# Eight places for late gate/up outputs, one product for the fifth class, gate/up grouped by side, and another written-out order

## The chip, the cores and the metric

The kernel runs on one core of one Trainium2 chip. The metric is the device time of one execution in microseconds. The core has five engines with an instruction queue each: PE (matrix products), ACT and DVE (elementwise work, and all copies out of PE's result memory, PSUM), POOL, and SP, which here only issues transfers.

## The reference

x is [2048, 640]; F is 1536. All arrays are bf16.

```python
xn = layernorm(x)                                   # over the 640 columns, no scale or shift
A  = irfft2(rfft2(xn) * (w_r + 1j * w_i))           # a filter in the two-dimensional spectrum
B  = ((xn @ w_gate) * (xn @ w_up)) @ w_down         # a bilinear gated layer, no activation
out = x + A + B
```

## The kernel before

**Blocks and names.** The 2048 rows are 16 blocks of 128. A block is normalised in place: statistics by two bn_stats and one aggregate on DVE (bn, ag), or by a sum and a sum of squares on ACT (sm at line 740, sq at line 749, for the blocks in `aset`: block 3 and blocks 6 to 15); then a square root on ACT (sd), a reciprocal and one tensor_scalar on DVE (rs, mul). Blocks 0 to 3 are transposed on PE (T0, line 818) and copied out (eT0); blocks 4 to 15 are transposed by a DMA on SP (xt).

**The gated layer.** A unit is a strip of one, two or four blocks and one or two column groups of 128 (ft 0 to 11). For each unit PE makes two GU tasks into one PSUM bank each (lines 948 and 968), ACT or DVE copies each out as bf16 (eG, lines 683 and 684), and one DVE product (H, lines 984 and 985) writes the hidden layer. There are 50 units, in the order of their readiness. The copies go to `GBF`, three places of two outputs in turn (`rr = ui % 3`), so an eG must wait for the H that read the place before. In units of four blocks one GU task is gate and the other up; in the smaller units each task computes gate and up for one column group.

**The spectrum.** DVE builds sums and differences of the normalised blocks in five groups (S1 to S5); PE turns them (R, line 908), ACT and DVE copy them out (eR). When all 16 are there, for each of 16 steps t: D (line 1025), its copy (eD), C (line 1045), the filter products WM on DVE with the weights of a group of two steps, negated copies NS on POOL, and, for each pair of steps, SM, JA and JB, then four inverse products IA (lines 1116, 1118) and their copies. WM has four products of 256 elements (line 1062) for classes one to four and two of 130 elements (line 1068) for the fifth class. Then 16 inverse steps I (line 1147) with copies eI, five DVE steps V1 to V5 for each of five groups of blocks, and the last transform IV (line 1236), which adds into the same PSUM bank as the down products ACC (line 1224).

**The end.** FINA copies a bank out on ACT, FIN adds x on DVE, SP stores. Block 15 is done in three pieces.

**Order.** Nothing is scheduled at run time. Every piece of work is a task; `_PLAN` lists all 976 as (number of the task in the order the code creates it, engine 0 to 4 = PE, ACT, DVE, POOL, SP, PSUM bank or -1). `replay` puts each engine's tasks in its queue in that order, and `compute_waits` derives the semaphore waits from buffers read and written. So each engine runs its list strictly in order, and a task that waits holds up all behind it on that engine. Gate load and x loads are issued by SP; the second half of block 0 and the up load of ft 0 and 1 by ACT. PE begins with 40 dummy products (`warm`) and, after T0_0, 12 small ones (`fill`).

**Buffers of filter weights.** The weights of two steps are loaded with 8 transfers (12 for the first) into one of three places; a place is free when the WM of its two earlier steps are done. The down weights (`WD`) lie over the table `TI`, which IA reads.

## Time and profile before

| what | value |
|---|---|
| median of 3 runs | 198.14 us (198.12 to 198.24) |
| span of the profiled execution | 196.1 us |
| PE busy | 191.5 us |
| DVE busy | 176.8 us |
| ACT busy | 136.7 us |
| POOL busy | 27.8 us |
| bytes moved by DMA | 23.75 MB |

The span goes from the first to the last instruction of the program on the core; the runs' time has some microseconds of start and end around it. Busy times of PE rest on modelled ends of its matmuls. A line number names the Python line that emitted the instruction; copies by ACT and DVE have one line each (683 and 684) whatever they copy.

### The profile page before, as it was taken

Reading aid. Unit: us, or ns where it says so; the run is one execution under the profiler, and the core shown is the slowest. Engines: PE = TensorE matmul, PEld = TensorE weight load, DVE = VectorE, ACT = ScalarE, POOL = GpSimd, SP = SyncE. Lnnn points to the kernel's source line nnn. Section 1 sums busy time; section 2 is a strip of 40 time slices with the busy share of each in tenths; the row PEclk is TensorE's granted clock in tenths of the full one; section 3 lists DMA queues with packets and bytes.
Section 4 is the critical chain, followed back from the end, with each engine's and each line's share of the span. In section 5 each row is a group of like instructions: output and inputs, shape, how many; then the busy total and the mean of one; then the engine's idle time right before and its main releaser. Section 6 shows DMA issues by size and latency. Waiting matters only on the chain.

```text
span 196.1 us, 4290 instructions
## 1 busy us (share of the span) xinstructions
PE 191.5 (98%) x1609; PEld 123.1 (63%) x1625; DVE 176.8 (90%) x392; ACT 136.7 (70%) x299; POOL 27.8 (14%) x54
## 2 busy tenths in 40 slices
PE   8999999999999999999999999999999999999995
PEld 8898645445454455556555556557777777777774
DVE  3899999999999889999899999994999999999823
ACT  3197999999957779999989999967505343333130
POOL 1000000000000004545172254460000000000000
PEclk9999999999999999999999999999999999999999
DMA  6999995426318432541451402004301334044422
GB/s 168 306 326 369 392 180 119 116 54 134 84 37 231 183 86 55 133 117 48 110 157 47 132 5 69 0 3 132 105 0 40 97 100 152 15 137 134 134 70 67
DMA packets 29667, 23.75 MB, mean 121 GB/s; under 512 B 10448, under 2 KB 27600, under 8 KB 29520
## 3 DMA queue, kind: packets, MB, share of 16 engines
q1 hardware_dynamic: 28848, 23.08, 41.6%
q10 hardware_dynamic: 800, 0.41, 0.7%
q8 instruction: 13, 0.21, 0.4%
q14 instruction: 6, 0.05, 0.1%
HBM read 18.89 MB, written 2.62 MB: 110 GB/s over the span
## 4 chain that ended last, share of the span: by engine, by line
PE 60%; DVE 19%; issue 6%; ACT 6%; SPq 4%; DMA 4%
PE ps L1224 27%; PE ps L948 21%; ACT arena L683 4%; SPq L677 4%; DMA arena<-in_A_x_dram 4%; DVE arena L984 3%; PE ps L1147 2%; DVE arena L861 2%; PE ps L1236 2%; PE ps L1025 2%; PE ps L1116 2%; PE ps L1045 2%; DVE arena L799 2%; DVE arena L860 2%; DVE arena L895 1%
## 5 line engine op out<-in xcount | busy, mean ns | idle before, releaser
L683 ACT ACTIVATE arena<-ps 128x512 bf16<-128x512 f32 (+6 forms) x243 | 117.3, 530 | 47.3 <-PE ps L1236 21.6
L948 PE MATMUL ps<-arena 128*128 128x512 bf16 x404 | 94.9, 379 | 0.9
L948 PEld LDWEIGHTS ps<-arena 128*128 128x128 bf16 x420 | 39.0, 98 | 41.1 <-ACT arena L683 0.9
L1224 PE MATMUL ps<-arena 128*128 128x320 bf16 (+2 forms) x396 | 57.2, 295 | 0.0
L1224 PEld LDWEIGHTS ps<-arena 128*128 128x128 bf16 x396 | 37.5, 98 | 13.4
L1062 DVE TENSOR_TENSOR arena<-ps,arena 128x256 bf16<-128x256 f32 x64 | 22.7, 418 | 1.4 <-PE ps L1045 1.1
L1077 POOL COPY arena<-arena 128x126 bf16<-128x126 bf16 x16 | 8.9, 556 | 104.1 <-DVE arena L1068 104.1
L984 DVE TENSOR_TENSOR arena<-arena 128x512 bf16<-128x512 bf16 x42 | 17.9, 425 | 0.5
L968 PE MATMUL ps<-arena 128*128 128x128 bf16 (+1 forms) x160 | 13.8, 246 | 0.0
L968 PEld LDWEIGHTS ps<-arena 128*128 128x128 bf16 x160 | 12.2, 98 | 1.3 <-issue 0.2
L1079 POOL TENSOR_SCALAR arena<-arena 128x130 bf16<-128x130 bf16 x16 | 11.8, 740 | 0.0
L1263 DVE TENSOR_TENSOR arena<-arena 128x640 bf16<-128x640 bf16 x15 | 7.1, 486 | 4.8 <-ACT arena L683 4.8
L740 ACT ACTIVATE arena<-arena 128x640 bf16<-128x640 bf16 x11 | 8.3, 757 | 3.6 <-DMA arena<-in_A_x_dram 3.6
L684 DVE CAST arena<-ps 64x321 bf16<-64x321 f32 (+4 forms) x16 | 8.3, 529 | 2.6 <-PE ps L1118 1.1
L1116 PEld LDWEIGHTS ps<-arena 128*128 128x128 bf16 x128 | 7.9, 120 | 3.0 <-issue 0.5
L749 ACT ACTIVATE arena<-arena 128x640 bf16<-128x640 bf16 x11 | 9.3, 844 | 0.0
L1025 PEld LDWEIGHTS ps<-arena 128*128 128x128 bf16 x160 | 7.1, 98 | 3.3 <-issue 0.2
L1116 PE MATMUL ps<-arena 128*128 128x64 bf16 x128 | 8.5, 199 | 0.0
L1068 DVE TENSOR_TENSOR arena<-ps,arena 128x130 bf16<-128x130 f32 x32 | 8.0, 295 | 0.0
L1025 PE MATMUL ps<-arena 128*128 128x64 bf16 (+1 forms) x160 | 8.0, 193 | 0.0
L860 DVE TENSOR_TENSOR arena<-arena 128x768 f32<-128x768 bf16 (+1 forms) x10 | 7.9, 792 | 0.0
L1078 POOL COPY arena<-arena 128x126 bf16<-128x126 bf16 x16 | 7.9, 495 | 0.0
(63 smaller groups left out, 201.2 us busy)
## 6 DMA issues: line engine op xcount, KB each, us to landing
arena<-in_A_x_dram SPq DMA_DIRECT2D x19, 160.0 KB, 2.6
arena<-in_A_w_r_dram SPq DMA_DIRECT2D x30, 80.2 KB, 2.2
arena<-in_A_w_i_dram SPq DMA_DIRECT2D x30, 80.2 KB, 2.2
out_dram<-arena SPq DMA_DIRECT2D x15, 160.0 KB, 1.8
arena<-in_B_w_gate_dram SPq DMA_DIRECT2D x4, 320.0 KB, 5.4
arena<-in_A_x_dram SPq DMA_DIRECT2D x1, 1280.0 KB, 10.1
arena<-c_tf SPq DMA_DIRECT2D x4, 256.0 KB, 10.3
arena<-c_ti SPq DMA_DIRECT2D x2, 512.0 KB, 5.3
```

Source lines behind the costliest of these rows:

```text
L683: return c.e.activation(dst, src, _ACTF.Copy)
L749: return c.e.activation(v_jk, v_x[:, b, :], _ACTF.Square, scale=-1.0, bias=v_m32[:, b:b + 1], accum_out=v_ss[:, b:b + 1])
L860: c.e.tensor_tensor(uo[:, o, :, 0:3, :], v_xb[:, b:b + nt, 0:6:2, :], v_xb[:, b:b + nt, 5:10:2, :], op)
L948: ins = c.e.matmul(ps[:, bk, :], v_gw[:, w, j, ft, :], v_xt[:, j, rows], start=(j == 0), stop=(j == 4))
L968: ins = c.e.matmul(ps[:, bk, w * n:(w + 1) * n], v_gw[:, w, j, ft, :], v_xt[:, j, rows], start=(j == 0), stop=(j == 4))
L984: return c.e.tensor_tensor(v_ht[:, ft0, rows], v_gbf[:, rr, 0, :], v_gbf[:, rr, 1, :], _OP.mult)
L1025: ins = c.e.matmul(ps[:, bk, k * 64:k * 64 + n], v_uq[:, k, t, :], v_fd[:, k * 128 + w * n: k * 128 + w * n + n], start=True, stop=True)
L1062: c.e.tensor_tensor(dst, xh, wv, _OP.mult)
L1077: c.e.tensor_copy(yg[:, :, 65:128], yg[:, :, 257:320])
L1079: return c.e.tensor_scalar(yg[:, :, 128:193], yg[:, :, 256:321], -1.0, None, _OP.mult)
L1116: c.e.matmul(ps[:, bk, 64 * k:64 * k + 64], yl[:, k:512:4], v_ti[:, q, 0, :], start=True, stop=True)
L1224: ins = c.e.matmul(ps[:, bk, 0:sl3.stop - sl3.start], v_ht[:, ft, a * 128:(a + 1) * 128], v_wd[:, ft, sl3], start=(ft == _FT_ORDER[0]), st ...
```

## The change

1. `GBF` keeps three places, and units of blocks 8 to 15 (24 of the 50) go through eight: three in `GBF` and five in the transposed input `XT`, columns 0 to 1023 of its five parts, which hold blocks 0 to 7. A copy to one of those five waits for all GU tasks of blocks 0 to 7.
2. In units of one and two blocks, one GU task now computes gate for both column groups and the other computes up; before, each computed gate and up for one group. H reads the two outputs accordingly.
3. WM's two products of the fifth class become one of 2 x 2 x 65 elements, with the spectrum broadcast over real and imaginary weights.
4. `act_set` becomes (2, 3): block 2's statistics go from DVE (bn, ag) to ACT (sm, sq). This leaves 975 tasks.
5. `fill` has 6 dummy products instead of 12.
6. `_PLAN` is new as a whole.

Parts of the new lists, by the names of the tasks (read from the task numbers), beside those of before:

```
ACT before: x0b, up(0,1), sd0, sd1, eT0_0, sm3, sd2, sq3, sd3, eG2_1, ...
ACT after:  x0b, up(0,1), sd0, sm2, sd1, sq2, eT0_0, sd2, sm3, sq3, sd3, eT0_2, eG2_0, ...
DVE before: ... ag1, mul0, rs1, mul1, eT0_0, eT0_1, eT0_1, eG0_0, eG0_1, H0, bn2, bn2, ag2, ...
DVE after:  ... ag1, mul0, rs1, mul1, eT0_0, rs2, eT0_1, mul2, eT0_1, eG0_0, eG0_1, H0, rs3, mul3, S1_0, ...
PE before:  warm, T0_0, fill, T0_1, GU0, GU0, GU2, GU1, GU1, GU3, GU2, GU3, T0_2, GU4, T0_3, GU4, ...
PE after:   warm, T0_0, fill, T0_1, GU0, GU0, T0_2, GU2, GU1, GU2, T0_3, GU1, GU3, GU3, GU5, GU5, GU4, ...
SP before:  x0a, x1, gate(0,1), gate(2,3), up(2,3), x2, x3, gate(4,5), up(4,5), gate(6,7), ...
SP after:   x0a, x1, x2, x3, gate(0,1), gate(2,3), up(2,3), x4-7, gate(4,5), sm, up(4,5), x8-15, gate(6,7), ...
DVE before: ... WM14, WM15, SM15, JB15, JA15, eIA28, eIA30, eI2, H47, V1_0, ...
DVE after:  ... WM14, WM15, SM15, JA15, JB15, H42, H43, eIA28, eIA31, eG49_0, H44, H45, eI2, H46, V1_0, ...
```

In the plan below, the first three lines of each list are shown.

```diff
@@ -358,6 +358,7 @@
 _S_GROUPS = ((0, 2), (2, 2), (4, 4), (8, 4), (12, 4))
 _V_GROUPS = ((0, 4), (4, 4), (8, 4), (12, 2), (14, 2))
 _NGW = 12
+_NG = 3
 _LAST = ((0, 320), (320, 512), (512, 640))
 _WD_LOADS = ((7, 12), (0, 2), (2, 4), (4, 6), (6, 7))
 _FT_ORDER = (7, 8, 9, 10, 11, 0, 1, 2, 3, 4, 5, 6)
...
-    (11, 4, -1), (12, 1, -1), (13, 4, -1), (171, 1, -1), (170, 4, -1), (8, 3, -1), (18, 2, -1), (172, 4, -1), (173, 4, -1),
-    (19, 2, -1), (20, 2, -1), (27, 2, -1), (28, 2, -1), (21, 1, -1), (14, 4, -1), (22, 2, -1), (29, 2, -1), (10, 0, 0),
-    (0, 3, -1), (30, 1, -1), (23, 2, -1), (24, 0, 2), (31, 2, -1), (32, 2, -1), (26, 2, -1), (25, 1, -1), (15, 4, -1),
...
+    (0, 3, -1), (10, 0, 4), (8, 3, -1), (11, 4, -1), (18, 2, -1), (12, 1, -1), (19, 2, -1), (20, 2, -1), (13, 4, -1),
+    (27, 2, -1), (28, 2, -1), (14, 4, -1), (15, 4, -1), (169, 4, -1), (170, 1, -1), (21, 1, -1), (36, 1, -1), (22, 2, -1),
+    (29, 2, -1), (23, 2, -1), (24, 0, 4), (9, 0, 1), (30, 1, -1), (37, 1, -1), (25, 1, -1), (31, 2, -1), (32, 2, -1),
...
@@ -559,7 +560,7 @@
         lay["TI"] = (lay["WD"][0], 16 * 256)
         b_g = alloc("G", 640)
         b_sm = alloc("SM", 384)
-        b_gbf = alloc("GBF", 6 * 512)
+        b_gbf = alloc("GBF", 2 * _NG * 512)
         b_stat = alloc("STAT", 608)
         b_jk = alloc("JK", 640)
 
@@ -617,7 +618,7 @@
         v_fd = V("FD")
         v_g = V("G")
         v_sm = V("SM").rearrange("p (t n) -> p t n", t=3)
-        v_gbf = V("GBF").rearrange("p (r u n) -> p r u n", r=3, u=2)
+        v_gbf = V("GBF").rearrange("p (r u n) -> p r u n", r=_NG, u=2)
         v_one = nc.const_aps.tensor(1.0, (128, 128), _BF)
         v_us = V("US").bitcast(_F32).rearrange("p (q j b) -> p q j b", q=8, j=5)
         v_tw = v_us[:, :, 1:3, :].rearrange("p q s b -> p s q b")
@@ -698,7 +699,7 @@
             return c.e.memset(v_eps, 1e-5)
         T("eps", "pool", 150.0, em_eps, writes=[(b_ve, None)], prio=-1.0)
         fills = []
-        nfill = opts.get("nfill", 12)
+        nfill = opts.get("nfill", 6)
 
         def em_fill(c):
             bk = bank_of(c.t)
@@ -731,7 +732,7 @@
                 [(b_x, ("s", b0, b0 + nb))], prio=(0.0, opts.get("x1_prio", 0.003), opts.get("x2_prio", 0.02), opts.get("x3_prio", 0.0205), 0.042, 0.06)[gi])
         muls = {}
         sd0 = None
-        aset = set(opts.get("act_set", (3,))) | set(range(opts.get("act_stats", 6), 16))
+        aset = set(opts.get("act_set", (2, 3))) | set(range(opts.get("act_stats", 6), 16))
         for gi, (b0, nb) in enumerate(_LN_GROUPS):
             pbase = 1.0 + 0.05 * gi if gi < 4 else opts.get("ln_prio", 5.9) + 0.05 * (gi - opts.get("ln_lead", 3))
             for b in range(b0, b0 + nb):
@@ -931,16 +932,22 @@
         c_at = [6.3 + opts.get("c_rate", 2.6) * (b0 + nb - 1) for b0, nb, _f0, _f1 in chunks]
         units = sorted((max(c_at[ci], w_at[ft | 1]), ci, ft) for ci in range(len(chunks))
                        for ft in range(chunks[ci][2], chunks[ci][3], 1 if chunks[ci][1] == 4 else 2))
+        gl = []
         for ui, (at_, ci, ft0) in enumerate(units):
             b0, nb = chunks[ci][:2]
             n = 128 * nb
             rows = slice(b0 * 128, b0 * 128 + n)
-            rr = ui % 3
+            late = [u_ for u_ in range(len(units)) if chunks[units[u_][1]][0] >= 8]
+            if ui in late:
+                rr = late.index(ui) % (_NG + 5)
+                rr = (rr + late[0]) % _NG if rr < _NG else rr
+            else:
+                rr = ui % _NG
+            gb = v_gbf[:, rr] if rr < _NG else v_xt[:, rr - _NG, 0:1024].rearrange("p (u n) -> p u n", u=2)
             pu = 40.0 + 0.005 * ui
             pe_ = opts.get("eg_prio", 5.0) + 0.001 * ui
             ph_ = opts.get("h_prio", 5.0) + 0.001 * ui
             for u in range(2):
-                ft = ft0 + u
                 if nb == 4:
                     def em_gu4(c, ft=ft0, w=u, rows=rows):
                         bk = bank_of(c.t)
@@ -953,37 +960,41 @@
                                   (b_xta, ("s", b0 * 128, b0 * 128 + n)), (b_xtb, ("s", b0 * 128, b0 * 128 + n))],
                            prio=pu + 0.001 * u, bank="single", cls="glu")
 
-                    def em_eg4(c, gu=gu, rr=rr, u=u):
-                        return copy_on(c, v_gbf[:, rr, u, :], ps[:, bank_of(gu), :])
+                    def em_eg4(c, gu=gu, gb=gb, u=u):
+                        return copy_on(c, gb[:, u, :], ps[:, bank_of(gu), :])
                     eg = T("eG_%d_%d" % (ui, u), ("act", "dve"), {"dve": _d_dve_psum(n), "act": _d_act(n)}, em_eg4,
-                           writes=[(b_gbf, ("r", 2 * rr + u, 2 * rr + u + 1))], prio=pe_, frees=gu)
+                           writes=[(b_gbf, ("r", 2 * rr + u, 2 * rr + u + 1))], after=gl if rr >= _NG else (), prio=pe_, frees=gu)
                     hold(gu, eg)
+                    if b0 + nb <= 8:
+                        gl.append(gu)
                     continue
 
-                def em_gu(c, ft=ft, n=n, rows=rows):
+                def em_gu(c, ft0=ft0, w=u, n=n, rows=rows):
                     bk = bank_of(c.t)
                     ins = None
-                    for w in range(2):
+                    for i in range(2):
                         for j in range(5):
-                            ins = c.e.matmul(ps[:, bk, w * n:(w + 1) * n], v_gw[:, w, j, ft, :],
+                            ins = c.e.matmul(ps[:, bk, i * n:(i + 1) * n], v_gw[:, w, j, ft0 + i, :],
                                              v_xt[:, j, rows], start=(j == 0), stop=(j == 4))
                     return ins
-                gu = T("GU_%d_%d" % (ft, b0), "pe", 10.15 * _d_mm(n), em_gu, after=fills,
-                       reads=[(b_gw, ("s", w_ * _NGW + ft, w_ * _NGW + ft + 1)) for w_ in range(2)] + [
+                gu = T("GU_%d_%d_%d" % (ft0, b0, u), "pe", 10.15 * _d_mm(n), em_gu, after=fills,
+                       reads=[(b_gw, ("s", u * _NGW + ft0, u * _NGW + ft0 + 2))] + [
                            (b_xta, ("s", b0 * 128, b0 * 128 + n)), (b_xtb, ("s", b0 * 128, b0 * 128 + n))],
                        prio=pu + 0.001 * u, bank="single", cls="glu2")
 
-                def em_eg(c, gu=gu, rr=rr, n=n, u=u):
-                    return copy_on(c, v_gbf[:, rr, u, 0:2 * n], ps[:, bank_of(gu), 0:2 * n])
+                def em_eg(c, gu=gu, gb=gb, n=n, u=u):
+                    return copy_on(c, gb[:, u, 0:2 * n], ps[:, bank_of(gu), 0:2 * n])
                 eg = T("eG_%d_%d" % (ui, u), ("act", "dve"), {"dve": _d_dve_psum(2 * n), "act": _d_act(2 * n)}, em_eg,
-                       writes=[(b_gbf, ("r", 2 * rr + u, 2 * rr + u + 1))], prio=pe_, frees=gu)
+                       writes=[(b_gbf, ("r", 2 * rr + u, 2 * rr + u + 1))], after=gl if rr >= _NG else (), prio=pe_, frees=gu)
                 hold(gu, eg)
-
-            def em_h(c, ft0=ft0, rr=rr, n=n, rows=rows, nb=nb):
+                if b0 + nb <= 8:
+                    gl.append(gu)
+
+            def em_h(c, ft0=ft0, gb=gb, n=n, rows=rows, nb=nb):
                 if nb == 4:
-                    return c.e.tensor_tensor(v_ht[:, ft0, rows], v_gbf[:, rr, 0, :], v_gbf[:, rr, 1, :], _OP.mult)
-                return c.e.tensor_tensor(v_ht[:, ft0:ft0 + 2, rows], v_gbf[:, rr, :, 0:n], v_gbf[:, rr, :, n:2 * n],
-                                         _OP.mult)
+                    return c.e.tensor_tensor(v_ht[:, ft0, rows], gb[:, 0, :], gb[:, 1, :], _OP.mult)
+                gu2 = gb[:, :, 0:2 * n].rearrange("p u (f n) -> p u f n", f=2)
+                return c.e.tensor_tensor(v_ht[:, ft0:ft0 + 2, rows], gu2[:, 0], gu2[:, 1], _OP.mult)
             T("H_%d" % ui, "dve", _d_dve_tt16(min(2 * n, 512)), em_h,
               reads=[(b_gbf, ("r", 2 * rr, 2 * rr + 2))],
               writes=[(b_ht, ("col", b0, b0 + nb))], prio=ph_)
@@ -1061,13 +1072,10 @@
                         dst = v_pr[:, w, 2 * pb:2 * pb + 2].rearrange("p g (h m k) -> p h g m k", h=2, k=4)[:, h]
                         c.e.tensor_tensor(dst, xh, wv, _OP.mult)
                 x5 = ps[:, bk:bk + 2, 256:321].unsqueeze(1).to_broadcast([128, 2, 2, 65])
-                d5 = v_y5[:, yr].rearrange("p g n -> p (g n)")[:, 0:648].rearrange("p (g n) -> p g n", g=2)
-                d5 = [d5[:, :, 256 * w:256 * w + 65] for w in range(2)]
-                ins = None
-                for w in range(2):
-                    ins = c.e.tensor_tensor(d5[w], ps[:, bk:bk + 2, 256:321], wt[:, w, :, 0:321:5], _OP.mult)
-                return ins
-            wm = T("WM_%d" % t, "dve", 1862.0, em_wm,
+                d5 = v_y5[:, yr]
+                d5 = bass.AP(d5.tensor, d5.offset, [d5.ap[0], [256, 2], [324, 2], [1, 65]])
+                return c.e.tensor_tensor(d5, x5, wt[:, :, :, 0:321:5], _OP.mult)
+            wm = T("WM_%d" % t, "dve", 1792.0, em_wm,
                    reads=[(b_wr[wr][0], ("r", b_wr[wr][1], b_wr[wr][1] + 16))],
                    writes=[(b_pr, ("r", pb, pb + 1)), (b_y5, ("r", 3 * yr, 3 * yr + 1))], prio=pq - 0.001, frees=tc)
             hold(tc, wm)
```

## The prediction

> **What bounds the kernel now.** I read the page first, then the chain that ended last, then the timelines of the first 22 us by engine, the waits, and the DMA issues. From the page:
>
> ```profile
> span 196.1 us, 4290 instructions
> ...
> PE 191.5 (98%) x1609; PEld 123.1 (63%) x1625; DVE 176.8 (90%) x392; ACT 136.7 (70%) x299; POOL 27.8 (14%) x54
> ...
> PEclk9999999999999999999999999999999999999999
> ```
>
> PE is busy 98% of the span at full clock, but ends of matmuls are modelled, so I count PE by start-to-start times. From the chain (start, length, what):
>
> ```profile
> 76.16 3.24 PE ps L948 x15
> ...
> 168.94 3.53 PE ps L1224 x26
> ```
>
> A 512-column matmul takes 3.24/15 = 0.216 us, a 320-column one 3.53/26 = 0.136; in the same way 256 columns take 0.109, 128 take 0.056, 321 take 0.137, and the 64-column ones 0.029 (L1025) and 0.033 (L1116, L1118). With the counts of the code, the work from the first gate/up product on is: gate/up 80 x 0.056 + 80 x 0.109 + 420 x 0.216 = 103.92; the last two transposes 0.56; R and I 160 x 0.056 = 8.96; D 4.64; C 4.38; IA 6.34; ACC 360 x 0.136 + 12 x 0.275 = 52.26; IV 4.36. Sum 185.42 us. The head of PE's timeline:
>
> ```profile
> 5.60 0.56 PE L818 MATMUL ps<-arena 128*128 128x128 bf16 x5 [0.35 <-DVE arena L799]
> 6.00 0.55 PE L707 MATMUL ps<-const-bfloat16-1.0 128*128 128x64 bf16 x12
> 6.39 0.44 PE L818 MATMUL ps<-arena 128*128 128x128 bf16 x5
> 6.84 4.79 PE L968 MATMUL ps<-arena 128*128 128x128 bf16 x80
> ```
>
> The first product starts at 6.84 and the last matmul (IV15_2) at 193.63, done at 193.69. So 186.85 us hold 185.42 of work: PE stands still only **1.43 us** after 6.84. By start times: 0.17 at 8.68 (second up load, landed 8.54), 0.12 at 11.86, 0.34 around 67.7 (R waits for S5_4), 0.19 and 0.15 at 80.8 and 81.7 (IA0, D5), 0.29 at 127.7 (C15), 0.22 at 134.6 (I0). The rest of the span is 2.45 us of last addition and store, and 6.84 us of head. The median of the runs is 2.0 us above the profiled span; I carry that over.
>
> So the kernel is PE's fixed work, plus the head, plus 1.43 us. A new order can only move the last two. Hence the head of ACT, which the new order changes:
>
> ```profile
> 1.23 0.46 ACTq L677 DMA_DIRECT2D arena<-in_B_w_up_dram  x1
> ...
> 5.27 0.29 ACT L775 ACTIVATE arena<-arena 128x1 f32<-128x1 f32 x1 [0.70 <-DVE arena L765]
> 6.20 0.38 ACT L683 ACTIVATE arena<-ps 128x256 bf16<-128x256 bf16 x1 [0.64 <-PE ps L818]
> 9.50 0.74 ACT L740 ACTIVATE arena<-arena 128x640 bf16<-128x640 bf16 x1 [2.92 <-DMA arena<-in_A_x_dram]
> 10.15 0.19 ACT L740 ACTIVATION_READ_ACCUMULATOR arena<-arena 128x1 f32 x1
> 10.24 0.28 ACT L775 ACTIVATE arena<-arena 128x1 f32<-128x1 f32 x1
> 10.43 0.81 ACT L749 ACTIVATE arena<-arena 128x640 bf16<-128x640 bf16 x1
> 11.14 0.19 ACT L749 ACTIVATION_READ_ACCUMULATOR arena<-arena 128x1 f32 x1
> 11.36 0.29 ACT L774 ACTIVATE arena<-arena 128x1 f32<-128x1 f32 x1
> ```
>
> The reader sees the two root steps and block 0's evacuation (6.20) done before the first sum on ACT (sm3, 9.50), which waits for its block of x. A sum holds ACT 0.74 us up to the next step, a square sum 0.93. And SP's first loads, from its timeline, with ACT's load from the DMA issues (last number: us to landing):
>
> ```profile
> 0.79 0.86 SPq L677 DMA_DIRECT2D arena<-in_A_x_dram  x2
> 1.71 0.99 SPq L677 DMA_DIRECT2D arena<-in_B_w_gate_dram  x2
> ```
>
> ```profile
> arena<-in_B_w_up_dram ACTq DMA_DIRECT2D x1, 320.0 KB, 3.9
> ```
>
> The up load of ACT's queue (1.23) lands 3.9 us later, at 5.18. SP's third load, issued at 1.71, lands at 6.31; by the trace's packets it begins at 4.2 to 4.6, on each engine as the up load ends there.
>
> [...] the trace at 3.7 to 4.2 us shows the up load alone though SP's third load was issued, so here issue order decides, with rival B left open. [...]
>
> **The change, part by part.**
>
> *Block 2's statistics to ACT.* DVE loses two bn_stats and one aggregate, 2 x 0.39 + 0.13 = 0.91 us. ACT gains 0.74 + 0.93 = 1.67. But the new ACT order is sd_0, sm2, sd_1, sq2, evacuation of T0_0. sm2 needs x block 2. In SP's new order that is the third load, issued at 1.71 behind ACT's up load: 5.18 plus its own 0.48 (block 3 landed 0.46 after block 2 before) gives at most 5.66; packet times of the up load's end (4.63) + 0.42 + about 0.45 give 5.5, which I take. Behind sm2 wait sd_1, then mul1 and T0_1; behind sq2 waits block 0's evacuation, and with it the first product:
> sm2 5.52; sd_1 +0.74 = 6.26 (before 5.27); sq2 +0.19 = 6.45; evacuation +0.93 = 7.38, ends 7.76 (before 6.58); first product +0.26 (as 6.58 to 6.84) = **8.02**, which is 1.18 later than 6.84. T0_1 comes at about 7.3 and is ahead of it. The first gate load, now fifth on SP, lands at 6.31 + 0.48 + 0.46 = 7.25 and does not bind.
>
> *Half the fill.* 6 x 0.032 = 0.19 us less on PE; it lies in the wait just named: worth nothing (0.19 if that wait were absent).
>
> *Grouping by side.* Same 160 matmuls, same evacuation sizes. It takes away the need for both weights in one task: the 0.17 at 8.68 goes. The H products have the same count and elements in another stride; no row shows that form, bounds 0 and (as f32) about 0.14 each for 8 of them, off the path; I take 0.
>
> *Five more places.* No wait of ACT for an H (L984) is in the list of waits, so nothing is removed directly; the places let the order put H later. They may be written only after every product of blocks 0 to 7, which PE has long passed then.
>
> *Merged fifth class.* Two 130-element products (295 ns, 0.21 start to start) become one of 260; nearest row L1062, 256 elements at 418 ns, 0.335 start to start. Saving between 0 and 0.09 each, 1.4 us at most of DVE in 16. DVE there has slack: the IA tasks start 0.3 to 8 us after their last input. Off the path: 0.
>
> *The order.* PE's work is the same 185.42. Against a PE that starts at 8.02, DVE sums: before, the end of S5 of each group is its DVE work plus a constant 5.2 to 5.6 us; the new queue has its mul3 at about 10.5 with 5.3 of work ahead, the same constant. Its S5_0 to S5_4 then end near 18.8, 25.4, 39.7, 53.4, 65.9; PE wants them at 19.6, 26.6, 41.2, 54.2, 67.2: the 0.34 goes. C15 wants eD15, near 124.8 on ACT, at 126.5: the 0.29 goes. IA0's group wants JA1 near 78.6 at 80.2: goes. I0 wants all of z2; eIA29 ends near 133.6, PE is there at 133.7: 0.17 stays. The weight loads are mixed on SP (part of group 10 waits behind group 12, hence for WM7; seven more issues of 0.46 and 1.8 of landing, against some 10 us of DVE up to WM10): covered. New: DVE puts H42 to H46 and one evacuation between JB15 and V1_0, 5 x 0.34 + 0.6 = 2.3 us, where before it stood idle 1.06, 1.03 and 0.55 us; V5_0 then ends near 146.9 for a PE that wants IV1_0 at 147.2 less 0.2 of hand-over, V5_4 near 159.1 for 159.2, V5_8 near 171.2 for 171.3. I allow 0.2 there and 0.1 elsewhere. Stalls after: 0.17 + 0.2 + 0.1 = 0.45 (0.1 to 1.2).
>
> *Sum (A).* 8.02 + 185.42 + 0.45 + 2.45 = 196.34 against 196.14, so +0.2: **198.3 us**, own range 197.9 to 198.8.
>
> **Rivals.**
> B, block 2 early: [...] x block 2 lands by 4.9, ACT releases the first product by 7.4, and the gate load binds instead: 7.25 + 0.14 = 7.39. With 0.3 of stalls: 0.55 - 1.43 + 0.3 = -0.58, 197.6 us. [...] against it: the order of packets at 3.7 to 4.2.
> C, slower, DVE late at the inverse: V1_0 after the deferred H. It decides once V1_0 starts later than about 136.6; each us beyond is a us of PE at IV1_0, since that sits in PE's queue. At 0.7 late: stalls 1.15, +0.9, 199.0 us. For it: margins of 0.1 to 0.3 at three hand-overs; against: the idle stretches of before.
> D, the clock falls: PE has work for only 0.7 us between 5.6 and 8.0. [...] 200.0 us. [...]
> E, the places remove a stall that I do not see: there are 1.43 us in all to be had; with a late head it is B's size at best.
>
> **From cases to numbers.** A 0.46, B 0.22 (E in it), C 0.25, D 0.07. What a measurement of this kernel can tell from no change is about 0.2%, 0.4 us. Faster: most of B and A's low end, 0.24; same: A's middle and edges of B and C, 0.43; slower: C, D and A's top, 0.33. Range 197.5 to 199.1: it holds B and C; D and the ends are left out.
>
> **What would show it.** First product near 8.0, with ACT's sum waiting for x until 5.5 (right) or starting before 5.0 (B). No PE gaps at 65 to 68 and at C15; small ones before IV at 147, 159, 171. A PEclk digit under 9 in the second slice means D. The prediction fails if the first product stands at 7.4 or before, or PE's stalls sum to over 1 us.

## The result, and the profile after

The changed kernel takes 198.70 us in the median of 20 runs (198.04 to 201.16), the kernel before 198.34 in 20 runs beside it: a ratio of 1.0016, 95 % interval 0.9995 to 1.0038. That is no change that can be measured, and the forecast of 198.3 is 0.4 us below it, its range of 197.5 to 199.1 holds it. But the 20 runs are not one cluster. By the clock that PE was granted on average, eleven had 1.0 (198.04 to 198.72, median 198.35), seven had 0.991 (199.36 to 199.87) and two 0.983 (200.81, 201.16; no profile shows these two). The forecast is the time of the first group; the other two are a rival that it gave 7 in 100. A median of this kernel therefore depends on how many of its runs fell into the groups with the lower clock.

The profiled execution (198.68 us, clock 1.0) shows the first group. From the page of the changed kernel:

```profile
span 196.5 us, 4241 instructions
...
PE 191.6 (97%) x1619; PEld 122.8 (62%) x1619; DVE 176.5 (90%) x375; ACT 137.4 (70%) x301; POOL 27.1 (14%) x54
```

PE's work is the same 191 us. The head of PE's timeline, then ACT's (start, length, engine, line, what, idle time before and what ended it):

```profile
6.68 0.45 PE L819 MATMUL ps<-arena 128*128 128x128 bf16 x5 [1.43 <-DVE arena L800]
6.97 0.35 PE L708 MATMUL ps<-const-bfloat16-1.0 128*128 128x64 bf16 x6
7.41 0.45 PE L819 MATMUL ps<-arena 128*128 128x128 bf16 x5
7.85 1.29 PE L977 MATMUL ps<-arena 128*128 128x128 bf16 x20
```

```profile
5.66 0.74 ACT L741 ACTIVATE arena<-arena 128x640 bf16<-128x640 bf16 x1 [0.93 <-DMA arena<-in_A_x_dram]
...
6.39 0.28 ACT L776 ACTIVATE arena<-arena 128x1 f32<-128x1 f32 x1
6.58 0.81 ACT L750 ACTIVATE arena<-arena 128x640 bf16<-128x640 bf16 x1
...
7.39 0.36 ACT L684 ACTIVATE arena<-ps 128x256 bf16<-128x256 bf16 x1
```

The chain is the predicted one: block 2's sum waits for its x (landed 5.63), the second root step and the square sum follow, and block 0's evacuation comes last on ACT, at 7.39; the first gate/up product starts at 7.85, which is 1.01 us later than before. PE ends later, too. Its last matmul, in the changed kernel and in the kernel before:

```profile
194.03 0.22 PE L1244 MATMUL ps<-arena 128*128 128x128 bf16 x1
```

```profile
193.63 0.22 PE L1236 MATMUL ps<-arena 128*128 128x128 bf16 x1
```

With PE's work between the two fixed at 185.36 us (the 185.42 of the prediction less the last matmul's 0.06), PE stood still for 194.03 - 7.85 - 185.36 = 0.82 us after the first product, against 1.43. Most of the 0.82 is one wait that was not forecast, before I12, the thirteenth inverse step. PE's timeline there, then ACT's:

```profile
162.14 0.30 PE L1244 MATMUL ps<-arena 128*128 128x320 bf16 x1
162.78 0.73 PE L1155 MATMUL ps<-arena 128*128 128x128 bf16 x10 [0.34 <-ACT arena L684]
```

```profile
159.82 0.77 ACT L684 ACTIVATE arena<-ps 128x320 bf16<-128x320 f32 x2 [1.12 <-PE ps L1244]
162.28 0.77 ACT L684 ACTIVATE arena<-ps 128x320 bf16<-128x320 f32 x2 [1.70 <-DMA out_dram<-arena]
```

By start times I12 comes 0.50 us late: it needs the bank that FINA of block 5 empties, and ACT waits 1.70 us to write that copy because the store of block 3, whose output place it reuses, has not landed. A smaller wait, 0.17 us, is that of R_8 at 54.34 for the end of DVE's sum S5_3 at 54.20. PE's timeline, then DVE's:

```profile
54.34 0.72 PE L909 MATMUL ps<-arena 128*128 128x128 bf16 x10
```

```profile
53.51 0.69 DVE L896 SCALAR_TENSOR_TENSOR arena<-arena 128x512 bf16<-128x512 f32 x1
```

The gaps at 67.7, at IA0, at D5 and at C15 are gone or under 0.1.

### The profile page after: what moved, and what is told of

Its sections match the earlier page's. It is cut to its first block, busy times and chain, and to the rows that moved or that the text cites. A ratio compares the mean times of both kernels' runs of the same rounds, so it can differ in the third digit from the quotient of the medians.

```text
span 196.5 us, 4241 instructions
## 1 busy us (share of the span) xinstructions
PE 191.6 (97%) x1619; PEld 122.8 (62%) x1619; DVE 176.5 (90%) x375; ACT 137.4 (70%) x301; POOL 27.1 (14%) x54
## 4 chain that ended last, share of the span: by engine, by line
PE 90%; DMA 4%; ACT 1%; DVE 1%; SPq 1%; issue 1%; ACTq 0%
PE ps L955 46%; PE ps L1232 22%; PE ps L977 7%; PE ps L1036 2%; PE ps L909 2%; DMA out_dram<-arena 2%; PE ps L1124 2%; PE ps L1056 2%; PE ps L1155 2%; DMA arena<-in_A_x_dram 2%; PE ps L1244 2%; SPq L678 1%; ACT arena L684 1%; PE ps L1126 1%; PE ps L819 1%
## 5 line engine op out<-in xcount | busy, mean ns | idle before, releaser
L955 PE MATMUL ps<-arena 128*128 128x512 bf16 x420 | 97.7, 379 | 0.0
L1232 PE MATMUL ps<-arena 128*128 128x320 bf16 (+2 forms) x396 | 57.2, 295 | 0.0
L685 DVE CAST arena<-ps 128x320 bf16<-128x320 f32 (+4 forms) x18 | 9.8, 556 | 2.0 <-PE ps L1126 0.6
L1087 POOL TENSOR_SCALAR arena<-arena 128x130 bf16<-128x130 bf16 x16 | 11.2, 700 | 0.0
L750 ACT ACTIVATE arena<-arena 128x640 bf16<-128x640 bf16 x12 | 10.4, 867 | 0.1
L741 ACT ACTIVATE arena<-arena 128x640 bf16<-128x640 bf16 x12 | 9.3, 772 | 0.9 <-DMA arena<-in_A_x_dram 0.9
L1244 PE MATMUL ps<-arena 128*128 128x320 bf16 (+2 forms) x33 | 7.9, 295 | 0.0
```

The lines of the kernel that those rows point to most:

```text
L685: return c.e.tensor_copy(dst, src)
L750: return c.e.activation(v_jk, v_x[:, b, :], _ACTF.Square, scale=-1.0, bias=v_m32[:, b:b + 1], accum_out=v_ss[:, b:b + 1])
L955: ins = c.e.matmul(ps[:, bk, :], v_gw[:, w, j, ft, :], v_xt[:, j, rows], start=(j == 0), stop=(j == 4))
L1087: return c.e.tensor_scalar(yg[:, :, 128:193], yg[:, :, 256:321], -1.0, None, _OP.mult)
L1232: ins = c.e.matmul(ps[:, bk, 0:sl3.stop - sl3.start], v_ht[:, ft, a * 128:(a + 1) * 128], v_wd[:, ft, sl3], start=(ft == _FT_ORDER[0]), st ...
L1244: return c.e.matmul(ps[:, bank_of(own), 0:sl3.stop - sl3.start], v_sm[:, 2, :], v_v[:, a, sl3], start=False, stop=True)
```

## The experiments

Throughout, "end" is the start of the last matmul and "stalls" is end - first gate/up product - 185.36, the sum that the prediction used. Edits of the plan are shown by task names in the engine's list.

### The changed kernel again, and what a second profile shows

> The changed kernel unchanged, profiled a second time. If ACT's sum of block 2 and the gate load set the head, as the prediction has it, the first gate/up product stands at 7.7 to 8.0 us again, whichever of x block 1 (5.16 in the first profile, 4.07 in the kernel before) and the first up load lands first. If instead the late x block 1 set it, the product moves to about 6.9 to 7.4 in a profile in which block 1 lands near 4.1. The 0.50 us stall before I12 at 162.8: if the order of DVE and SP makes it, it is there again (0.4 to 0.5, store of block 3 landing after 162); if it was the accident of a slow store (4.04 us from issue to landing), it is under 0.15 and the span is 196.0 to 196.1.

199.09 us in the median of 15 runs (ratio 1.0035, 1.0016 to 1.0054). Eight of the 15 had a granted clock of 0.991 (199.05 to 200.39), seven had 1.0 (198.46 to 199.09). The profiled execution is one of the eight. The first product stands at 8.12, a little above the 7.7 to 8.0 that was expected, although x block 1 landed at 4.46 in it: so the head is set by ACT's sum and what follows it, as forecast, and not by block 1. The sum started at 5.92 here, because block 2 landed at 5.90. The I12 stall is there again, 0.62 us, the store landing at 164.02, 4.17 us after its issue. And PE is at half clock right after the first product. Its timeline, which is to be held against 7.85 1.29 above:

```profile
6.27 0.35 PE L708 MATMUL ps<-const-bfloat16-1.0 128*128 128x64 bf16 x6
7.67 0.45 PE L819 MATMUL ps<-arena 128*128 128x128 bf16 x5 [1.05 <-DVE arena L800]
8.12 2.21 PE L977 MATMUL ps<-arena 128*128 128x128 bf16 x20
```

The trace's clock record switches at 4.83, 8.24 and 11.65, every 3.41 us. Cut there, the windows read (from:to, length, busy time of PE with its instructions, of the weight loads, DVE, ACT and POOL, then the granted clock):

```profile
1.42:4.83 3.41, 3.41 (x34) 3.41 (x33) 1.44 (x4) 1.58 (x2) 0.00 (x0) 1.00 0.85 221
4.83:8.24 3.41, 1.50 (x23) 1.07 (x22) 1.98 (x9) 2.32 (x8) 0.00 (x0) 1.00 1.13 324
8.24:11.65 3.41, 3.41 (x35) 3.41 (x34) 2.61 (x9) 2.60 (x6) 0.00 (x0) 0.50 1.10 346
```

(No clock record covers the first window; its 1.00 is not to be trusted, since its matmuls start 107 ns apart as in the third, where products of the same size at full clock start 56 ns apart.) The second row shows what went before the loss, and the third its price: PE worked for 1.50 of 3.41 us while it waited for ACT, and got half clock for the whole next window, which holds 35 matmuls instead of about 60. That the first caused the second is tested next.

### Keep the clock up, and see what is left

```diff
-        nfill = opts.get("nfill", 6)
+        nfill = opts.get("nfill", 24)
...
-        nwarm = opts.get("nwarm", 10)
+        nwarm = opts.get("nwarm", 12)
```

> The changed kernel with more dummy products and nothing else: 48 instead of 40 in the warm-up ahead of the first transpose, 24 instead of 6 between the first two transposes. Theory D (found in the second profile of the changed kernel: PE ran at half clock from 8.22 to 11.69 us because it had done only about 1 us of work in the 3.4 us before): the granted clock is 1.0 in nearly all runs instead of 0.991 in half of them, no stretch at half clock after the first gate/up product, and the median falls to that of the runs with a full clock, 198.4 to 198.8. Rival (the clock falls whatever PE does there, from an earlier state): 0.991 stays in a third or more of the runs and the median stays at 199.0 to 199.5.

198.25 us (198.02 to 198.42), 12 of 12 runs with 0.999 or more; ratio 0.9986 (0.9970 to 1.0003). The theory holds. The window that begins at full clock, in the same columns:

```profile
5.17:8.58 3.41, 2.69 (x52) 2.26 (x51) 1.88 (x10) 2.64 (x8) 0.00 (x0) 1.00 1.14 307
```

The first product is no earlier (8.13), but the stalls after it are 193.78 - 8.13 - 185.36 = 0.29 us. So the new order at full clock costs 1.29 us ahead of the first product and returns 1.14 behind it.

Is it the halved fill of the change that lost the clock? Two runs put it back, or take it from the kernel before:

```diff
 the changed kernel:                  the kernel before:
-nfill 6                              -nfill 12
+nfill 12                             +nfill 6
```

> The changed kernel with 12 dummy products between the first two transposes again, as before the change; all else as after. Theory D1 (halving the dummy products made the clock fall): 0.2 us more of PE work in the window is enough, the granted clock is 1.0 in nearly all runs, median 198.3 to 198.6. Theory D2 (the late first gate/up product made it fall, 1.0 us less of work in the window; the dummy products are a small part): 0.991 stays in a third to a half of the runs, median 198.6 to 199.3. The kernel before with only the new head has 12 dummy products and fell in 11 of 20 runs, which speaks for D2.

198.73 us, ratio 1.0027 (1.0007 to 1.0048); seven of 20 runs at 0.991.

> The kernel before with 6 dummy products instead of 12, nothing else. If the late head makes the clock fall and not the dummy products: first product near 6.7 to 6.9, granted clock 1.0 in all runs, median within 0.2 of before. Rival (the dummy products carry the clock): 0.991 in a third or more of the runs, median 0.3 or more above before.

198.33 us, ratio 1.0005 (0.9990 to 1.0020); no run of 16 under 0.999, first product 6.74. So the late product loses the clock, and 0.2 us of dummy products doesn't decide it. (The runs don't settle whether the twelve make the loss somewhat rarer. With six it was 9 of 20 and 8 of 15 here, and 14 of 20 in the run with a store moved, below, whose head is the same.)

PE's busy time in the window that began at full clock, for the profiles that lost the clock and for four of those that kept it:

| kernel | window | PE busy | next window |
|---|---|---|---|
| store moved (below) | 3.82 to 7.23 | 1.49 | half |
| changed, second profile | 4.83 to 8.24 | 1.50 | half |
| changed, 12 dummies | 3.97 to 7.39 | 1.60 | half |
| changed, first profile | 5.33 to 8.74 | 1.97 | full |
| before, new head, more dummies | 3.62 to 7.03 | 2.65 | full |
| changed, more dummies | 5.17 to 8.58 | 2.69 | full |
| before | 5.88 to 9.29 | 3.39 | full |

In the five other profiles whose window covers the head PE was busy for 2.58 us or more, and the next window was at full clock. So in these profiles the border lies between 1.60 and 1.97 of 3.41 us. The windows lie differently against the program from run to run, and so cut the same kernel differently (1.50 and 1.97 in the two profiles of the changed kernel). This accounts for its losing the clock in some runs and not in others, about half.

The 129 runs of the kernel before that stood beside the experiments had an average clock of 0.999 or more without exception. Twelve of them took 199.15 to 200.04 us all the same. The average can hide a half clock early in the program, as the next profile shows, and what those twelve lost is open. No run gave the kernel before more dummy products.

### The new head alone

On the kernel before: block 2's statistics from DVE to ACT, and the queues

```diff
-ACT: sd0, sd1, eT0_0, sm3, sd2, sq3, sd3, ...
+ACT: sd0, sm2, sd1, sq2, eT0_0, sm3, sd2, sq3, sd3, ...
-SP:  x0a, x1, gate(0,1), gate(2,3), up(2,3), x2, x3, ...
+SP:  x0a, x1, x2, x3, gate(0,1), gate(2,3), up(2,3), ...
-DVE: ..., H0, bn2, bn2, ag2, eG1_1, ...
+DVE: ..., H0, eG1_1, ...
```

> The kernel before with only the new head: block 2's statistics on ACT in the changed kernel's order (root, sum, root, square sum, evacuation), none of them on DVE, and x blocks 2 and 3 ahead of the first gate load on SP. Theory 1: first product at 7.85 (+1.0); second up load lands near 9.9 and holds PE by 0.2 again; DVE is relieved of 0.91 us, so the 0.34 us before R_14 goes; the end moves by 1.0 less 0.3 to 0.5: span 196.6 to 196.9 against 196.1. Rival (the head's loss is only the race of x block 1 against the up load, or DVE rather than PE sets the middle): the first product is later by 1.0, but the stalls take nearly all of it up, span 196.0 to 196.3.

200.28 us, ratio 1.0069 (1.0050 to 1.0088); eleven of 20 runs at 0.991. The profile has the first product at 8.26 and half clock until 10.26, so its span of 197.9 misses the expected 196.6 to 196.9 by the clock, which I had not priced. (Its average clock is printed as 1.000 nevertheless, and its run of 199.90 us is the slowest of the nine with that average.) With the clock held up by the same 48 and 24 dummy products:

> The kernel before with the new head alone, and with 48 and 24 dummy products so that the clock stays up: what the head costs at full clock, without the new middle. If the order of the middle and end is what gives the 1 us back: first product near 8.1, no stretch at half clock, and the end 0.5 to 1.0 later than before: median 198.8 to 199.3. Rival (the old middle takes the late head up as well, DVE being relieved of block 2's 0.91 us): within 0.3 of before, 198.1 to 198.6.

199.25 us, ratio 1.0050 (1.0032 to 1.0067), clock 1.0 in all four. First product at 8.16, which is 1.32 later than before; stalls 194.42 - 8.16 - 185.36 = 0.90 against 1.43, end 0.79 later. So the old middle absorbs 0.5 of a late head (the waits at 8.68, 11.86 and 67.7 are gone, those at IA0, D5, C15 and I0 stand), and about 0.8 us reach the end. The kernel with the whole new order and the same dummy products has the same head and 0.29 of stalls. The new middle is thus worth 0.6 us by the ends (194.42 to 193.78), and 0.9 by the medians, each against the kernel before beside it (+0.82 and -0.08). The prediction's balance, a head that costs and a middle that returns it, is right in sign and in mechanism.

### Can the early product be had with the new middle?

Two tries to put the old head before it. In the first, on the changed kernel:

```diff
-ACT: sd0, sm2, sd1, sq2, eT0_0, sd2, sm3, ...
+ACT: sd0, sd1, eT0_0, sm2, sq2, sd2, sm3, ...
-SP:  x0a, x1, x2, x3, gate(0,1), ...
+SP:  x0a, x1, gate(0,1), x2, x3, ...
-DVE: eT0_0, rs2, eT0_1, mul2, eT0_1, eG0_0, eG0_1, H0, rs3, ...
+DVE: eT0_0, eT0_1, eT0_1, eG0_1, eG0_0, H0, rs2, mul2, rs3, ...
-PE:  T0_1, GU0_0, GU0_1, T0_2, GU2_0, GU1_0, GU2_1, T0_3, GU1_1, GU3_0, GU3_1, GU5_1, ...
+PE:  T0_1, GU0_1, GU0_0, GU2_1, GU2_0, GU1_0, GU1_1, T0_2, GU3_0, GU3_1, T0_3, GU5_1, ...
```

> The changed kernel with its head undone: on ACT the second root step and block 0's evacuation ahead of block 2's two sums, on SP the first gate load ahead of x blocks 2 and 3, on PE the up side first, and the transposes of blocks 2 and 3 after six and eight gate/up products instead of two and five; all else as after. Theory 1 (ACT's sums ahead of the evacuation cost about 1 us at the first product and buy an early block 3 for DVE): first product at 6.8 to 7.0 if x block 1 lands near 4.1, 7.6 if it lands at 5.2; block 3's multiply moves from 10.25 to about 11.1, so the S groups come up to 0.8 us later, and R_0, R_2, R_8, R_15 (slack 0.50, 0.34, 0.15, 0.15) give 0.3 to 0.7 us back as stalls: span 196.0 to 196.5 against 196.5. Rival (the head is PE's alone): the whole gain reaches the end, span 195.5 to 195.8.

199.89 us, ratio 1.0070 (1.0043 to 1.0097), clock 1.0. The first product is at 6.92, as theory 1 has it, but neither theory's price is right: the end is at 195.84. Block 3's multiply starts at 11.38 (10.17 in the changed kernel's first profile, 10.45 in that with more dummies), and with it move T0_3 and everything that PE could do next. PE's timeline of this run:

```profile
10.58 1.28 PE L977 MATMUL ps<-arena 128*128 128x128 bf16 x20
12.34 0.45 PE L819 MATMUL ps<-arena 128*128 128x128 bf16 x5 [0.48 <-ACT arena L684]
13.91 3.44 PE L977 MATMUL ps<-arena 128*128 128x256 bf16 x30 [1.11 <-ACT arena L684]
18.17 2.02 PE L977 MATMUL ps<-arena 128*128 128x256 bf16 x17 [0.83 <-ACT arena L684]
```

After eight gate/up products the work of blocks 0 and 1 with the weights at hand is used up; then PE stands for blocks 2 and 3 and for banks that ACT empties late. The stall before I12 is in this run as well, 0.59 us. Part of the waiting is my choice of banks, so this run doesn't show the least that such a head must cost.

In the second try everything up to the fifth unit is as in the kernel before (statistics of block 2 on DVE, gate loads first), with the store of block 3 moved:

```diff
-the changed kernel's lists up to GU5
+the lists of before up to eG4_1, with GU1_0 ahead of GU1_1; then the changed kernel's
```

> The changed kernel's middle and end (with the store of block 3 moved ahead) behind the head of the kernel before: block 2's statistics on DVE, the root steps and the evacuation ahead of ACT's sums, gate loads ahead of x blocks 2 and 3, 12 dummy products only as the changed kernel's code sets them (6), PE's first 16 tasks in the order of before. Theory 1 (head and middle are separate): first product at 6.84, full clock, and the stalls of the changed kernel's middle (0.4 without I12), span 195.0 to 195.4. Rival (the two heads trade: an early first product is paid with late blocks 2 and 3 on DVE, so that the R tasks wait): first product at 6.84, but R_0, R_2, R_8 and R_15 stall by 0.5 to 1.1 in all, span 195.7 to 196.2.

199.66 us, ratio 1.0070 (1.0055 to 1.0085). The rival is right, and by more than it said: the product is at 7.00, but PE's timeline has

```profile
20.91 0.72 PE L909 MATMUL ps<-arena 128*128 128x128 bf16 x10 [1.88 <-DVE arena L896]
```

R_0 comes 2.04 us late by start times. DVE works without a break from block 3's multiply at 12.23 (10.45 in the changed kernel with more dummies) to the end of the first S group. So the two heads do trade: x blocks 2 and 3 early mean late gate weights and an ACT that is full, gate weights early mean a late block 3 on DVE, and it is block 3 that starts DVE's chain S1 to S5, which leaves no slack: in the changed kernel R_8 already waits for S5_3.

### The late store

On SP, in the changed kernel, one step moves:

```diff
-SP: ..., st2, ld_xr6, ld_xr7, st3, ...
+SP: ..., st3, st2, ld_xr6, ld_xr7, ...
```

> The changed kernel with one step moved: the store of block 3 ahead of the store of block 2 and of the loads of blocks 6 and 7 on SP. Theory: the store waits behind them by 1.8 us, and its late landing (162.26) holds ACT for 1.70 us and so I12 for 0.50 us; with the move it is issued near 156.0 and lands near 158, ACT's wait is gone, PE's stall before I12 is under 0.1 and the span is 196.0 to 196.1. Rival (the stall was a slow store only, or moves to the next wait): I12 stands where it stands in the unchanged kernel of the same call, span within 0.15 of it.

The stall before I12 is gone. In ACT's timeline the wait in the same place is now for PE:

```profile
161.06 1.58 ACT L684 ACTIVATE arena<-ps 128x320 bf16<-128x320 f32 x4 [1.12 <-PE ps L1244]
```

But this run's own span, 197.3, is not the expected 196.1: it was at half clock from 7.23 to 10.65, and 14 of its 20 runs had 0.991 (199.48 us, ratio 1.0030, 1.0012 to 1.0049). Its six runs at 1.0 have a median of 198.31. With the clock held up as well:

> The same with the store of block 3 moved ahead as well. If the two losses are separate and add up: 0.5 to 0.6 us below the kernel with more dummy products alone, 197.8 to 198.3, at or a little below the kernel before; no stall before I12. If only one of them reaches the end, within 0.2 of the better of the two.

198.28 us, ratio 0.9997 (0.9987 to 1.0007): nothing beyond the dummy products alone. The profiles say why: with more dummies and the old order of stores the store of block 3 landed 1.96 us after its issue (160.43), in time; there was no I12 stall left to remove. In the three profiles with the stall it took 4.04, 4.14 and 4.17 us. What lies between is a transfer of 16 KB of instructions, one packet of 1.09 us in the first of them: at 159.37, 161.30 and 161.36 in those three, just behind the issue of the store (157.8, 159.4, 159.5), and at 155.50 with 26 more instructions in PE's list. So the order made the store 1.8 us late, and the place of an instruction transfer seems to have decided whether that cost 0.5 us or nothing. With 12 dummy products it came at 158.57, the store landed 2.29 us after the start of its issue, and I12 didn't wait. That is a coincidence in times and not shown as a cause: no run moved the instruction transfer alone.

### The merged product alone

```diff
...
-                for w in range(2):
-                    ins = c.e.tensor_tensor(d5[w], ps[:, bk:bk + 2, 256:321], wt[:, w, :, 0:321:5], _OP.mult)
-                return ins
+                return c.e.tensor_tensor(d5, x5, wt[:, :, :, 0:321:5], _OP.mult)
```

> The kernel before with only the two fifth-class products merged into one of 2 x 2 x 65. By the prediction's step: 0 to 0.09 us less on DVE in each of 16, 1.4 at most, nothing at the end: median within 0.2 of before. Rival (DVE sets the middle, the WM stage among it): the stalls of PE at IA0, D5 and C15 (0.19, 0.15, 0.29) shrink and the end comes 0.3 to 0.6 earlier.

198.16 us, ratio 0.9984 (0.9970 to 0.9997), at the edge of what can be told from no change. DVE's timeline of one step, in this run and in the kernel before:

```profile
104.55 0.45 DVE L1066 TENSOR_TENSOR arena<-ps,arena 128x260 bf16<-128x260 f32 x1
104.90 1.08 DVE L984 TENSOR_TENSOR arena<-arena 128x512 bf16<-128x512 bf16 x2
```

```profile
104.53 0.50 DVE L1068 TENSOR_TENSOR arena<-ps,arena 128x130 bf16<-128x130 f32 x2
104.94 1.08 DVE L984 TENSOR_TENSOR arena<-arena 128x512 bf16<-128x512 bf16 x2
```

To the start of what follows it is 0.35 us with the merged product and 0.41 with two: DVE saves 0.06 in such a step, inside the prediction's 0 to 0.09. Of the three gaps that the rival named, the one before D5 (0.15) is gone, those at IA0 and at C15 stand. The stalls of the profile are 193.68 - 6.82 - 185.36 = 1.50 against 1.43 all the same, since the waits at the start are longer in it (0.31 and 0.15 where the kernel before has 0.17 and 0.12). So the rival is right about one small gap, and no gain at the end is shown.

### A head that waits for neither

The runs above say what a better head needs: an early product, x block 3 early on DVE, and no thin window for the clock. In the changed kernel DVE idles for 1.1 us after block 0's multiply (1.14 with more dummies, 1.07 with the store moved; not in the first profile, where x block 1 landed late), waiting for the second root step, which sits behind the sum on ACT though its input is there. So block 2's statistics go back to DVE, into that gap:

```diff
-ACT: sd0, sm2, sd1, sq2, eT0_0, sd2, sm3, sq3, sd3, eT0_2, ...
+ACT: sd0, sd1, eT0_0, sm3, sq3, sd2, sd3, eG2_1, ...
-DVE: ..., mul1, eT0_0, rs2, eT0_1, mul2, eT0_1, eG0_0, eG0_1, H0, rs3, mul3, S1_0, ...
+DVE: ..., mul1, eT0_0, bn2, bn2, ag2, eT0_1, eT0_1, eG0_1, eG0_0, rs2, mul2, rs3, mul3, H0, S1_0, ...
-PE:  T0_1, GU0_0, GU0_1, T0_2, GU2_0, GU1_0, GU2_1, T0_3, ...
+PE:  T0_1, GU0_1, GU0_0, GU2_1, GU2_0, GU1_0, T0_2, T0_3, ...
-warm 40, st2 ... st3
+warm 48, st3, st2
```

> The changed kernel with a head that waits for neither: block 2's statistics on DVE, in the 1.1 us in which it stands idle after block 0's multiply, the second root step and block 0's evacuation ahead of ACT's sum of block 3, the up side first on PE, the transposes of blocks 2 and 3 after five gate/up products, x blocks 2 and 3 still early on SP, 48 dummy products in the warm-up, store of block 3 moved ahead. Theory (DVE's chain from block 3's multiply to the S groups and PE's first product must both come earlier for the end to move): first product at 7.0 to 7.2 at full clock, block 3's multiply ends near 10.0 instead of 10.8, S groups 0.4 to 0.8 us earlier, span 195.3 to 195.8 against 196.1, 197.4 to 197.9 in the median. Rival (DVE has no idle time to give: the 0.9 us of statistics push the S groups back, as in the run with the head of before): R tasks stall by 0.8 or more, span 196.1 or above.

197.62 us (197.00 to 198.04), ratio 0.9968 (0.9957 to 0.9979): 0.3 % faster than before with an interval clear of 1, and clock 1.0 in all ten. The profiled execution is the slowest of the ten (span 195.9), and already has the first product at 7.37 and block 3's multiply at 10.00. From ACT's timeline:

```profile
6.87 0.38 ACT L684 ACTIVATE arena<-ps 128x256 bf16<-128x256 bf16 x1 [0.76 <-PE ps L819]
7.15 0.73 ACT L741 ACTIVATE arena<-arena 128x640 bf16<-128x640 bf16 x1
```

The evacuation that came last on ACT now comes ahead of the sum. The end is at 193.40, stalls 0.67: PE again waits 0.17 at R_8, for DVE. By this account the head could be earlier still, but only together with DVE's chain; no run shows that.

## Why the prediction was right, and where it was not

**First product at 8.02.** Measured 7.85 and 8.12; at full clock with more dummies 8.13. Sum of block 2 at 5.52: 5.66, and 5.94 with more dummies. In the first profile the root step and the square sum came as worked out (+0.73, +0.19), the evacuation 0.12 sooner (+0.81), and from its end to the product it took 0.10 instead of 0.26. The gate load, which "lands at 7.25 and does not bind", landed at 7.80 in the first profile, 0.05 ahead of the product: there it bound as much as ACT did, whose evacuation ended at 7.75. In the other profiles of the changed kernel with this head it landed at 7.30 to 7.95.

**Stalls after, 0.45.** Right in sum at full clock without the I12 stall: 0.29 and 0.32 in the two runs with more dummies. (The terms 0.17, 0.2 and 0.1 add up to 0.47, not 0.45.) The 0.34 at R_14, the second up load, IA0, D5 and C15 went; I0 keeps 0.06 instead of 0.17; the hand-overs at IV1_0, IV4_0 and IV8_1, for which 0.2 was allowed, cost nothing.

The margin given to DVE's sums was too wide. S5_0 to S5_4 were to end near 18.8, 25.4, 39.7, 53.4 and 65.9; they ended at 19.02, 26.24, 40.52, 54.20 and 67.26, while PE came to the R tasks at the times forecast (19.51, 26.57, 41.16, 54.34, 67.40). So the fourth sum makes PE wait 0.17 where 0.8 to spare was forecast, and the wait at R_14 shrank under 0.1 with nothing left of the 1.3 that were forecast. That the sum of stalls came out near 0.45 is thus in part luck. The two tries at an early head show what the missing margin means.

Missing from the list is I12, 0.50. The prediction had looked at the deferred H42 to H46 and at V1_0, rival C, and at the products behind it, but not at what the order does to stores on SP, where two loads and the store of block 2 went ahead of the store of block 3. By its own sign of being wrong, stalls of over 1 us, the first profile is within (0.82) and the second is not (195.79 - 8.12 - 185.36 = 2.31, of which half clock and I12 are nearly all).

**The sum, A.** 8.02 + 185.42 + 0.45 + 2.45 = 196.34, hence 198.3. Runs at full clock: 198.35; with the clock held up 198.25. Case A gives the time that the change has when the clock stays.

**Rival D, and the step in it that failed.** That the clock would hold through the gap, and so 0.07, was my estimate, which no trace had shown. PE had been busy for 44 to 47 % of a window of 3.41 us, and ran at half clock in the next one. Its share in the runs was 9 of 20, 8 of 15 and 14 of 20 for kernels with this head, and 7 of 20 with 12 dummies. Its size was too large as well: its 200.0 us, my estimate too, stands 1.7 above the 198.3 of case A, and the four profiles with a late half-clock window have 0.9 to 1.4 us more of stalls than those without (the stall before I12 set aside), in three of them because PE has no product to make in part of the window, and because a later PE no longer waits for DVE at R_8; the runs took 199.4 to 199.9 in place of 200.0.

The measured median of 198.70 is the mean of the two slowest of the eleven runs at full clock (198.69 and 198.72). With two fewer of these among the 20 it would have been 199.37, above the range; in the 15 runs measured later, with seven, it was 199.09, at the range's upper end. So the forecast's number was right by its likeliest case, and the median stayed with that case by luck: the estimate that the clock would hold failed, and just over half of these runs kept it. The range was wide for other reasons, rivals B and C.

**Half the fill, "worth nothing".** Right for time, by the runs with 12 and with 6; the reason given, that it lies in the wait, leaves out that PE's busy time there also bears on the clock. Grouping by side and the merged product: 0 at the end as said, but only the merged product was measured alone. What the grouping does is not shown: the wait at the second up load, which it was to take away, is also gone in the kernel before with the new head alone, which has no such grouping. The five places alone were not tried.

**Rivals B and C.** B (x early) is out: the sum started at 5.66 or later each time. The loads of two queues did run side by side: in the first profile packets of SP's x loads and of ACT's up load start in every 0.1 us from 3.4 to 4.6, and x block 1 and the up load landed together, at 5.16 and 5.20. But block 2, next on SP, landed at 5.63 all the same. C's hand-overs held; a deferred H (H47, 0.34 us ahead of the additions of blocks 3 and 2) only added to the lateness of a store.

## What to carry to other kernels

Where PE's head has a thin stretch, count its busy time in 3.41 us before deciding what a late product costs: where it was about half or less (1.60 of 3.41 us), the next 3.41 us ran at half clock, in some executions and not in others, and 26 more dummy products repaired it here. A step put early on a full in-order engine is paid by what waits behind it (with more dummies T0_0's products started on PE at 5.90 and took 0.45, and ACT copied them out at 7.67, behind block 2's sum and square sum); look for an idle engine that can take it, here DVE in the gap of 1.1 us that the same step had made. When an order moves work past a queue of transfers, follow the stores too: a place that comes free late can make another engine wait, as ACT did here for 1.70 us, for a store on SP.

## What the runs showed of the hardware

In these profiles the clock changed at multiples of 3.41 us whose phase against the program differed by run: at 4.83, 8.24 and 11.65 in the second profile of the changed kernel, at 5.33 and 196.48 in its first and at 5.88 and 197.02 in the kernel before, both 191.15 apart, which is 56 times 3.413. At half clock 128-column products start 107 ns apart, at full clock 56. For the way up, a window at half clock with PE busy 2.72 us (3.43 to 6.84, new head alone) did not raise it; one with 2.79 (0.20 to 3.62, new head with more dummies) and one with 3.06 (2.47 to 5.88, kernel before) did. In the profile of the new head alone the average granted clock was still printed as 1.000, since the record begins where the clock first rose, at 10.26: the matmuls' start times show the half clock that the average hides.

By busy time the border on the way up (2.72 to 2.79) is thus another than on the way down (1.60 to 1.97). But at half clock a product keeps PE busy about twice as long (107 ns against 56). Counted in columns, of the products that start in a window, the same windows fall on the two sides of one border: 2688 or fewer at full clock lost it (changed kernel, 12 dummies) and 3712 kept it (changed kernel, first profile); at half clock 3200 did not raise it (0.02 to 3.43, new head alone) and 3328 did (2.28 to 5.69, merged product alone). No run tells which of the two is counted.

Two loads issued within 40 ns of each other on SP and ACT (18 ns in the kernel before, 28 in the first profile of the changed kernel) landed together or a microsecond apart: x block 1 (160 KB) and the first up load (320 KB) at 4.07 and 5.18 in the kernel before, 5.16 and 5.20 in the changed kernel's first profile, 4.46 and 5.51 in its second.

A store of 160 KB landed 1.45 us after the end of its issue when alone (first profile of the changed kernel, issued from 162.84 to 163.18, landed at 164.63) and took 4.04 to 4.17 us behind two loads and an instruction transfer.
